# K's exponentials read from PSUM, stores of x's parts on another queue, weight blocks loaded shifted

## The chip, the cores and the metric

The kernel runs on one core of a Trainium2 chip. The metric is the device time of one execution in microseconds (us). TensorE (PE) multiplies, VectorE (DVE) and ScalarE (ACT) do arithmetic on tiles in SBUF and PSUM, GpSimd (POOL) and SyncE (SP) mostly issue DMA transfers. A name such as L457 is a line of the kernel, of the one before where nothing else is said; lines of the changed kernel lie a little further down (L457 before and L464 after are the same store).

## The reference, cut to what matters

```python
def phi(x):                                  # q, k: [8, 8, 576, 64], w_phi: [64, 128]
    proj = np.einsum('bhsd,df->bhsf', x, w_phi)
    proj = proj - np.max(np.abs(proj), axis=-1, keepdims=True)
    return np.concatenate([np.exp(proj), np.exp(-proj)], axis=-1)
q_p, k_p = phi(q), phi(k)
kv  = np.einsum('bhsf,bhsd->bhfd', k_p, v)
z   = np.sum(k_p, axis=2)
num = np.einsum('bhsf,bhfd->bhsd', q_p, kv)
den = np.einsum('bhsf,bhf->bhs', q_p, z)[..., None] + 1e-06
x   = (num / den).transpose(0, 2, 1, 3).reshape(4608, 512)

gate = 1.0 / (1.0 + np.exp(-(x @ w_gate)))   # w_gate, w_val: [512, 1536]
val  = x @ w_val
out  = (gate * val) @ w_out                  # w_out: [1536, 512]
```

A linear attention makes x, and a gated two-layer network takes x to the output. For each token (a row of 576 per head) the largest absolute value over its 128 features is taken off its projection before the exponentials of both signs. The network's weights arrive as 64-bit floats.

## The kernel before, in words

**Attention.** There are 32 steps, one for each batch and pair of heads (`attend`). A step loads q, k and v, projects K on TensorE with tokens on the partitions (L489, four 128x128 products for each of two heads) and Q with features on the partitions (L594). VectorE takes each K token's largest absolute value (L495, `mk`, one number per token). Then, for K, VectorE subtracts it from the 512 columns of a group in PSUM and writes `ek` in SBUF (L524), and ScalarE takes two exponentials of 512 elements per group, one of each sign (L536). A step has two such groups of 128x512 and a small one for the last 64 tokens. TensorE then sums K with V (L678) and multiplies by Q; VectorE's transposes (L637, L644) carry Q's maxima across partitions. Ratios of numerator and denominator, multiplied out by L809, are x, feature-major, written to the scratch `xs` in DRAM. For the first chunk of 512 tokens x is kept in SBUF and split there into a high and a low part: ScalarE writes the high part (L815), VectorE the low one (L818), four parts of 128 features each.

**First phase of the network.** x has nine chunks of 512 tokens. For the first four of the twelve blocks of 128 hidden features, each chunk goes through gate and value products (`gate`, L997: twelve matmuls of 128x512, since high and low parts give three products for each of four slices), a nonlinearity, a split of h in high (L1021) and low part, and four output products (L1054, `go` in `first_js`: twelve matmuls each, three for each of the four hidden blocks). Chunks 0 to 6 take tanh and an exponential for the sigmoid; chunks 7 and 8 take the Sigmoid function (L1017), whose table is loaded once, behind all of ScalarE's work ahead. The output product leaves PSUM through ScalarE (L1077) into one of two y buffers, from which a store (L1083) on SP's queue writes it to `out`. For chunks 1 to 8 `load_x` fetches x from `xs`, splits it, and `keep_x` (L457) stores its high and low parts to `xh` and `xl` in DRAM, for the second phase: 144 stores on SP's queue.

**Weights.** A block of weights, 128x512 numbers of 64 bits, is loaded as 32-bit words, from which VectorE and ScalarE put together high and low parts with bit operations. `weigh` does this: L855 masks, ScalarE rescales (L859), and L874, L882, L894, L911 and L946 shift, combine and multiply. There are twelve blocks for the first phase, and 24 more for the second, whose sums (`kept`) are written to DRAM scratch, partly between attention steps, partly later.

**Second phase.** The other eight blocks of hidden features go by a seven-product scheme (products of sums of blocks) over blocks of 768 tokens: L1283 multiplies, and POOL adds the results onto `out` by accumulating stores (L1437). Its first loads of x's parts (L1215) wait until all of x's parts, `xh` and `xl`, are stored.

**What sets the order.** Every operation is given to a planner (`Plan`) with its engine, a modelled duration, a rank and its buffers. The planner plays the program through with these durations and issues the operations of each engine in the order that comes out. Each engine then works strictly in that order, and a queue's transfers too. So a change of a rank, of a duration or of a count moves work on all engines. Gate products have PSUM banks of their own (three, named gate below) and attention five (named bank).

Of the kernel before, what the change touches and what calls it, by code (L numbers as in the profile page):

```python
# [8 lines left out]
F32 = mybir.dt.float32  # L9
F32R = mybir.dt.float32r  # L10
U32 = mybir.dt.uint32
# [34 lines left out]
ONPE = 12  # L46
BANKS = 5
# [4 lines left out]
WAT = 0.0  # L52
WSTEP = 6.0
# [13 lines left out]
SLACK = 12.0  # L67
LAG = 0.0
ISSUE = 0.4
# [3 lines left out]
SHARE = 0.33  # L73

# [87 lines left out]
class Plan:  # L162
# [5 lines left out]
    RATE = 0.26, 0.36  # L168
# [24 lines left out]
    def run(self):  # L193
# [33 lines left out]
        while left:  # L227
# [25 lines left out]
            free[o.eng] = t + max(o.busy, ISSUE if late and o.eng == "SP" else 0.0)  # L253
# [40 lines left out]
def attention_moe(  # L294
# [126 lines left out]
    def on_act(n, fn, reads, writes, rank, after=(), slack=0.0):  # L421
        return plan.op(
            "ACT", 0.08 + n / 1200, 0.17, fn, reads, writes, rank, None, slack, after
        )
# [26 lines left out]
    def keep_x(c, p, bufs, r):  # L451

        for n, x in enumerate(bufs):
            for t, w, of in pieces(c * CW, CW):
                sp(
                    w * 512,
                    lambda n=n, x=x, t=t, w=w, of=of: nc.sync.dma_start(  # L457
# [7 lines left out]
    def attend(i):  # L465
# [63 lines left out]

        for g in range(3):  # L530
            n = (4, 4, 1)[g] * F
            dve(n, lambda g=g: k_sub(g), [(pk[0], pk[1], pt)[g], mk[g]], [ek[g]], r + 4 + g)
# [54 lines left out]
        else:  # L587
# [59 lines left out]
            on_act(2 * S, lambda: act.activation(e(), d(), AF.Exp), [d], [e], r + 14)  # L647
# [190 lines left out]
    def weigh(j, m, r, deep, wh, wl, ms, part, after=(), again=False, whole=None):  # L838
        raw = Buf([r_raw2 if again else r_raw], [P, 2 * DM])
        top = Buf([r_top2 if again else r_top], [P, DM])  # L840

        def words(x):
            return x().rearrange("p (n two) -> p n two", two=2)

        def hi():
            return words(raw)[:, :, 1]

        sp(
            512 << 10,
            lambda: nc.sync.dma_start(raw(), w_moe[j, :, m, :].bitcast(U32)), [], [raw], r,  # L850
            after,
        )
        dve(
            DM,
            lambda: vec.tensor_scalar(top(), hi(), 0x7FFFFE00, None, op0=ALU.bitwise_and),  # L855
            [raw], [top], r, k=2.0,
# [3 lines left out]
            [], [top], r,  # L860
        )
        if deep:
            mid = Buf([r_mid], [P, 2 * DM])
            sp(
                512 << 10,
                lambda: nc.sync.dma_start(
                    mid()[:, : 2 * DM - 1].bitcast(U16),
                    w_moe[j, :, m, :].bitcast(U16)[:, 1 : 4 * DM - 1],
                ),
                [], [mid], r,  # L870
            )
            dve(
# [694 lines left out]
```

## Time and profile before

| | before |
|---|---|
| three runs, us | 1167.53, 1165.16, 1164.63 (median 1165.16) |
| the profiled execution, us | 1164.72 |
| its span in the profile, us | 1163.0 |
| mean granted TensorE clock | 0.994 |
| TensorE busy, us | 1134.9 (98%), 8940 matmuls |
| VectorE busy, us | 925.3 (80%), 1805 instructions |
| ScalarE busy, us | 712.7 (61%), 1425 instructions |
| POOL busy, us | 77.9 (7%), 94 instructions |
| DMA bytes moved | 213.37 MB, 183 GB/s on average |

The profile is of one execution; busy times are sums over the records of an engine, and issuing a DMA from SP isn't counted as busy. "Idle before" is the time that an engine stood still ahead of an instruction, with the releaser, the piece of work whose end let it go on. SPq is SP's DMA queue. The granted clock is TensorE's speed as the throttle allowed it, 1.00 being full speed.

### The profile page before, as it was taken

The numbers are of one execution on the slowest core, as the hardware profiler recorded it, in microseconds if no ns is written. First come the engines' busy times: TensorE is split into PE (matmuls) and PEld (weight loads), VectorE is DVE, ScalarE is ACT, GpSimd is POOL, SyncE is SP. The second block draws the span as 40 slices with busy tenths as digits, with TensorE's granted clock in tenths as the row PEclk, the third lists the DMA queues.
The fourth block names the chain that finished last, engine by engine and source line by source line (L and its number), as shares of the span: only waits on it lengthen the run. The fifth ranks groups of instructions, "written<-read, shape, count | busy, mean of one in ns | idle before, by whom it ended". The sixth has DMA issues, their size and how long they took to land.

```text
span 1163.0 us, 23394 instructions
## 1 busy us (share of the span) xinstructions
PE 1134.9 (98%) x8940; PEld 952.9 (82%) x8940; DVE 925.3 (80%) x1805; ACT 712.7 (61%) x1425; POOL 77.9 (7%) x94
## 2 busy tenths in 40 slices
PE   8989999999999999999989999999999999999998
PEld 6656666766676776767768999999999999999998
DVE  7998889999999999978687956756767766667665
ACT  6857676665767666553344756656567666566563
POOL 0000000000000000000000112012022022022020
PEclk9989999999999999999989999999999999999999
DMA  6773466555738548375867558468495667567671
GB/s 237 236 252 101 134 216 203 167 194 185 242 111 259 183 144 264 115 242 184 324 239 261 152 106 212 144 125 216 148 249 124 172 122 202 165 123 195 171 165 55
DMA packets 114712, 213.37 MB, mean 183 GB/s; under 512 B 21544, under 2 KB 59560, under 8 KB 114600
## 3 DMA queue, kind: packets, MB, share of 16 engines
q1 hardware_dynamic: 101928, 177.27, 46.3%
q0 software_dynamic: 12672, 34.61, 16.9%
q8 instruction: 70, 1.15, 0.4%
q14 instruction: 42, 0.34, 0.1%
HBM read 126.61 MB, written 85.07 MB: 182 GB/s over the span
## 4 chain that ended last, share of the span: by engine, by line
PE 71%; DVE 16%; DMA 7%; ACT 2%; issue 2%; SPq 2%; DVEq 0%; ACTq 0%
PE bank L1283 29%; PE gate L1283 15%; PE gate L997 8%; PE gate L1054 4%; PE bank L678 3%; DMA rb<-den 3%; PE bank L720 2%; PE bank L489 2%; DMA low<-xs 1%; PE bank L1054 1%; DVE mb L637 1%; PE bank L738 1%; PE bank L594 1%; DVE pm L616 1%; PE bank L997 1%
## 5 line engine op out<-in xcount | busy, mean ns | idle before, releaser
L1283 PE MATMUL bank<-low,high 128*128 128x384 f32 x1338 | 246.8, 336 | 0.0
L1283 PEld LDWEIGHTS bank<-low,high 128*128 128x128 f32 x1338 | 233.3, 188 | 0.9 <-DVE flat L1304 0.4
L997 PE MATMUL gate<-low 128*128 128x512 f32 x708 | 173.8, 399 | 5.4 <-ACT low L815 4.3
L997 PEld LDWEIGHTS gate<-low 128*128 128x128 f32 x708 | 131.9, 191 | 36.3 <-ACT low L815 4.8
L1283 PE MATMUL gate<-low,high 128*128 128x384 f32 x678 | 130.9, 336 | 0.6 <-ACT gate L1298 0.6
L1283 PEld LDWEIGHTS gate<-low,high 128*128 128x128 f32 x678 | 118.6, 188 | 1.1 <-ACT gate L1298 1.1
L1283 PE MATMUL bank<-low 128*128 128x384 f32 x523 | 116.8, 339 | 1.2 <-DVE spare L1304 1.0
L536 ACT ACTIVATE ek<-ek 128x512 f32<-128x512 f32 (+1 forms) x192 | 95.4, 528 | 26.5 <-DVE ek L524 25.5
L1283 PEld LDWEIGHTS bank<-low 128*128 128x128 f32 x523 | 92.7, 188 | 4.4 <-DVE spare L1304 1.3
L1054 PE MATMUL gate<-low 128*128 128x512 f32 x372 | 89.4, 394 | 0.0
L1382 ACT CAST low<-flat 128x384 fp32r<-128x384 f32 x126 | 62.8, 515 | 40.2 <-DVE flat L1391 36.7
L1054 PEld LDWEIGHTS gate<-low 128*128 128x128 f32 x372 | 68.5, 188 | 14.7 <-issue 1.0
L1437 POOL DMA_DIRECT2D out<-third x60 | 52.7, 1177 | 350.8 <-DVE third L1304 266.2
L678 PE MATMUL bank<-ek,vin 128*32 128x256 f32 x1240 | 73.2, 381 | 2.2 <-ACT d L607 2.2
L1304 DVE TENSOR_TENSOR flat<-bank,flat 128x384 f32<-128x384 f32 x74 | 40.4, 554 | 40.9 <-PE bank L1283 34.1
L678 PEld LDWEIGHTS bank<-ek,vin 128*32 128x32 f32 x1240 | 37.5, 110 | 41.6 <-issue 5.6
L1391 DVE TENSOR_TENSOR flat<-flat,bank 128x384 f32<-128x384 f32 x39 | 21.4, 550 | 61.2 <-PE bank L1283 61.2
L1437 POOL DMA_DIRECT2D out<-spare x22 | 19.4, 881 | 686.5 <-DVE flat L1376 662.9
L1283 PE MATMUL gate<-low 128*128 128x384 f32 x267 | 65.1, 338 | 0.0
L1385 DVE TENSOR_TENSOR low<-flat,low 128x384 fp32r<-128x384 f32 x108 | 58.8, 551 | 1.8 <-ACT low L1382 0.6
L1298 ACT COPY bank<-bank 128x384 f32<-128x384 f32 x81 | 37.8, 467 | 33.7 <-PE bank L1283 32.2
L1021 ACT CAST low<-flat 128x512 fp32r<-128x512 f32 x36 | 22.3, 619 | 53.0 <-DVE flat L1046 41.4
(213 smaller groups left out, 2181.4 us busy)
## 6 DMA issues: line engine op xcount, KB each, us to landing
out<-third POOLq DMA_DIRECT2D x60, 384.0 KB, 8.2
flat<-w_moe SPq DMA_DIRECT2D x28, 512.0 KB
low<-xh SPq DMA_DIRECT2D x33, 384.0 KB
low<-xl SPq DMA_DIRECT2D x33, 384.0 KB
low<-xs SPq DMA_DIRECT2D x33, 384.0 KB
kin<-k SPq DMA_DIRECT2D x32, 320.0 KB
qin<-q SPq DMA_DIRECT2D x32, 320.0 KB
vin<-v SPq DMA_DIRECT2D x32, 320.0 KB
```

What stands on the lines that cost most here:

```text
L489: nc.tensor.matmul(pk[hd]()[:, t, :], x()[head(hd), t * P : t * P + P], wk[head(hd), :], start=True, stop=True,)
L536: lambda g=g, sg=sg: act.activation(ek[g]()[:, :, sg * F : sg * F + F], ek[g]()[:, :, F:], AF.Exp, scale=1.0 - 2.0 * sg,),
L678: nc.tensor.matmul(o_[o : o + Q, : 2 * F], vx()[:, 2 * t + hd, o % D : o % D + Q], (e0, e1)[hd][:, t, :] if t < 4 else e2[:, 0, :], start= ...
L720: nc.tensor.matmul(nm()[o : o + Q, :], w()[:, sg, o : o + Q], es[sg]()[:, o // D, cs], start=sg == 0, stop=sg == 1, tile_position=(0, o),)
L997: nc.tensor.matmul(o(), a()[:, ws], x(), start=cc + n == 0, stop=cc == NC4 - 1 and n == 2,)
L1054: nc.tensor.matmul(acc(), w()[:, ms], a(), start=first and i == 0, stop=last and i == 2)
L1283: nc.tensor.matmul(o()[:, :HT], s()[:, ws], y, start=first and n + cc + i_ == 0, stop=n == len(terms) - 1 and cc == steps - 1 and i_ == 2, ...
L1298: HT, lambda: act.copy(o()[:, :HT], src()[:, :HT]), [src], [o], -200.0, before
L1304: HT, lambda: vec.tensor_tensor(at_(), p()[:, :HT], q(), op=ALU.add),
L1382: on_act(HT, lambda: act.copy(hh(), y()), [y], [hh], -100.0, after)
L1385: lambda: vec.tensor_tensor(hl(), y(), hh().bitcast(F32), op=ALU.subtract),
L1437: lambda f=f, y=y: nc.gpsimd.dma_start(final(f, dc), flat_y(y), accum_op=ALU.add),
```

## The change

It does five things, and changes some of the planner's durations and ranks besides.

1. From step 12 on (20 of the 32 steps), K's two large groups are no longer subtracted by VectorE. ScalarE reads the projection in PSUM and takes the exponential with the token's maximum as its bias, one ACTIVATE for each of four slices of 128 elements and each sign. VectorE writes the negated maxima (128x4).
2. `keep_x`'s 144 stores go through POOL's queue instead of SP's.
3. The 24 weight blocks for sums are loaded shifted by two bytes (the host pads each row by one number to allow it), so that one word holds what two words held; each block needs one combining operation of VectorE less.
4. The weights of the first phase have ranks of their own: gate and value blocks of all four hidden blocks ahead, the output blocks later. Which blocks are loaded a second time at another offset (`deep`) follows from that position.
5. For the last three chunks (`PARTED`) an output product is cut in two, three hidden blocks first (nine matmuls) and the fourth by itself (three).

```diff
-WAT = 0.0
-WSTEP = 6.0
+WG = 0.0
+WGS = 6.0
+WO = 72.0
+WOS = 6.0
...
+PARTED = 3
...
-ISSUE = 0.4
+ISSUE = 0.43
...
                 sp(
-                    w * 512,
-                    lambda n=n, x=x, t=t, w=w, of=of: nc.sync.dma_start(
+                plan.op(
+                    "POOL", 1.0, w * 512,
+                    lambda n=n, x=x, t=t, w=w, of=of: nc.gpsimd.dma_start(
...
+        def k_exp(g, sg):
+            for t in range(4):
+                act.activation(
+                    ek[g]()[:, t, sg * F : sg * F + F], pk[g]()[:, t, :], AF.Exp,
+                    bias=(mn, mk)[sg][g]()[:, t : t + 1], scale=1.0 - 2.0 * sg,
+                )
+
+        mn = [at(f"mq{g}", 2, [P, 4]) for g in range(2)]
         for g in range(3):
             n = (4, 4, 1)[g] * F
+            if i >= FUSED and g < 2:
+                plan.op(
+                    "DVE", 0.1, 0.16,
+                    lambda g=g: vec.tensor_scalar(mn[g](), mk[g](), -1.0, None, op0=ALU.mult),
+                    [mk[g]], [mn[g]], r + 4 + g,
+                )
+                for sg in range(2):
+                    plan.op(
+                        "ACT", 1.12, 0.17, lambda g=g, sg=sg: k_exp(g, sg),
+                        [pk[g], (mn, mk)[sg][g]], [(ek[g], sg)], r + 6 + g,
+                    )
+                continue
...
+    def weighed(j, m, r, mask, rings, after=(), slack=0.0, deep=True, o=1):
...
+                lambda x=x, o=at_: nc.sync.dma_start(
+                    x().bitcast(U16), w_moe[j, :, m].bitcast(U16)[:, o : o + 4 * DM]
                 ),
...
+    def weigh_whole(j, m, r, w, ms, part, after, early):
+
+        top, raw, mid = weighed(
+            j, m, r, 0x7FFF0000, (r_raw, r_top, r_raw) if early else (r_raw2, r_top2),
+            after, LATER, early and DEEP,
+        )
...
-            def go(t=t, acc=acc):
-                for i in range(JA):
-                    mm_out(acc, t, hs[i], i, i == 0, i == JA - 1)
...
+            for a, b in ((0, JA - 1), (JA - 1, JA)) if c >= NCH - PARTED else ((0, JA),):
+
+                def go(t=t, acc=acc, a=a, b=b):
+                    for i in range(a, b):
+                        mm_out(acc, t, hs[i], i, i == 0, i == JA - 1)
...
-                i, WAT + 3 * WSTEP * i, WSTEP, lambda m, i=i: 3 * i + m >= RAW, (r_wh, r_wl, r_oh, r_ol),
+                i, lambda m, i=i: WO + WOS * i if m == 2 else WG + WGS * (2 * i + m),
+                lambda m, i=i: (8 + i if m == 2 else 2 * i + m) >= RAW, (r_wh, r_wl, r_oh, r_ol),
```

How the work is ordered then, at three places. Each row is a line, an operation and its tiles, output<-input, with the output's shape; "x12" is so many in a row. First VectorE, where the first chunk's x gets its last low parts (L818 before, L845 after). Before:

```order
L946 SCALAR_TENSOR_TENSOR low<-flat 128x512
L855 TENSOR_SCALAR flat<-flat 128x512
L809 TENSOR_TENSOR xp_623<-ex_391,mb_678 128x576
L495 TENSOR_REDUCE mk_217<-bank_164 128x4
L882 SCALAR_TENSOR_TENSOR flat<-flat 128x512
L809 TENSOR_TENSOR xp_840<-ex_688,rb_517 128x576
L818 TENSOR_TENSOR low<-xp_623,low 128x512
L637 STREAM_TRANSPOSE mb_678<-pm_558 128x1152
L818 TENSOR_TENSOR low<-xp_840,low 128x512
```

After the change:

```order
L836 TENSOR_TENSOR xp_518<-ex_687,rb_478 128x576
L836 TENSOR_TENSOR xp_763<-ex_365,mb_700 128x576
L653 COPY pn_667<-pm_646 64x36
L654 COPY pn_667<-pm_646 64x36
L655 TENSOR_TENSOR pm_646<-pm_646,pn_667 128x36
L658 COPY pn_667<-pm_646 32x36 x4
L659 TENSOR_TENSOR pm_646<-pm_646,pn_667 128x36
L845 TENSOR_TENSOR low<-xp_518,low 128x512
L845 TENSOR_TENSOR low<-xp_763,low 128x512
L664 STREAM_TRANSPOSE mb_700<-pm_646 128x1152
```

Between the two divisions (L809, L836) and the low parts, work on a weight block has been replaced by small work on Q's maxima (L653 to L659), and the transpose (L637, L664) now stands behind both low parts. Second SP's queue, where chunk 6's outputs are stored. Before:

```order
L457 DMA xh<-low 128x128
L457 DMA xh<-low 128x384
L457 DMA xl<-low 128x128
L457 DMA xl<-low 128x384
L1083 DMA out<-flat 128x512 x2
L850 DMA more<-w_moe 128x1024
L1123 DMA g_98<-flat 128x1792
L850 DMA more<-w_moe 128x1024
L1083 DMA out<-flat 128x512 x2
```

After the change:

```order
L1002 DMA low<-xs 128x128
L1002 DMA low<-xs 128x384
L1119 DMA out<-flat 128x512 x4
L875 DMA more<-w_moe 128x2048 x2
L1159 DMA g_100<-staged 128x1792
L875 DMA more<-w_moe 128x2048 x2
L1252 DMA flat<-xs 128x768
```

The stores of x's parts ahead of the outputs (L1083, L1119) are gone, and the four outputs are together, behind loads of x (L1002). Third TensorE, from the last gate or value product of chunk 6 to those of chunk 7. Rows that read from high,low are chunk 7's; the rows of L1054 (L1087 after) ahead of them are chunk 6's output products. Before:

```order
L997 MATMUL gate_191<-low 128x512 x12
L997 MATMUL bank_176<-high,low 128x512 x12
L1054 MATMUL gate_178<-low 128x512 x12
L1054 MATMUL gate_185<-low 128x512 x12
L1054 MATMUL gate_191<-low 128x512 x12
L1054 MATMUL gate_178<-low 128x512 x12
L997 MATMUL bank_154<-high,low 128x512 x12
L997 MATMUL bank_166<-high,low 128x512 x12
```

After the change, from chunk 6's last two output products to chunk 7's first two:

```order
L1087 MATMUL gate_178<-low 128x512 x12
L1087 MATMUL gate_185<-low 128x512 x12
L1030 MATMUL bank_164<-high,low 128x512 x12
L1030 MATMUL bank_176<-high,low 128x512 x12
L1030 MATMUL bank_150<-high,low 128x512 x12
L1030 MATMUL bank_166<-high,low 128x512 x12
L1030 MATMUL bank_152<-high,low 128x512 x12
L1030 MATMUL gate_191<-high,low 128x512 x12
L1030 MATMUL gate_178<-high,low 128x512 x12
L1030 MATMUL gate_185<-high,low 128x512 x12
L1087 MATMUL bank_164<-low 128x512 x9
L1087 MATMUL bank_176<-low 128x512 x9
```

A whole output product is a row of x12, and of a parted one the first piece is x9. Before, one product of chunk 7 (bank_176) stood ahead of chunk 6's output products; now all eight stand behind them, and two pieces of x9 come next, ahead of the pieces that need the fourth hidden block.

More of the change, by code (lines that the diff above doesn't have):

```diff
@@ L67 @@
 SLACK = 12.0
+PARTED = 3
+LATER = 0.0
+DEEP = False
 LAG = 0.0
-ISSUE = 0.4
+ISSUE = 0.43
 SPAN = 46.0
@@ L252, in run @@
                     b.slot.take()
-            free[o.eng] = t + max(o.busy, ISSUE if late and o.eng == "SP" else 0.0)
+            free[o.eng] = t + max(o.busy, ISSUE if o.eng == "SP" else 0.0)
             if o.eng in ("SP", "POOL"):
@@ L419, in dve, with on_act @@
         )
[L421 removed]
+    def on_act(n, fn, reads, writes, rank, after=(), slack=0.0, k=1.0):
         return plan.op(
[L423 removed]
+            "ACT", 0.08 + n / 1200 / k, 0.17, fn, reads, writes, rank, None, slack, after
         )
@@ L836, in attend, with words @@
             t += wd
[L838 to L843, printed above, removed]
-        def hi():
[L846 to L852, printed above, removed]
-        dve(
-            DM,
-            lambda: vec.tensor_scalar(top(), hi(), 0x7FFFFE00, None, op0=ALU.bitwise_and),
-            [raw], [top], r, k=2.0,
+    def words(x, n):
+        return x().rearrange("p (n two) -> p n two", two=2)[:, :, n]
+    def weighed(j, m, r, mask, rings, after=(), slack=0.0, deep=True, o=1):
+        raw, top = Buf([rings[0]], [P, 2 * DM]), Buf([rings[1]], [P, DM])
+        mid = Buf([rings[2]], [P, 2 * DM]) if deep else raw
+        for x, at_ in ((raw, 0), (mid, 1)) if deep else ((raw, o),):
+            sp(
+                512 << 10,
+                lambda x=x, o=at_: nc.sync.dma_start(
+                    x().bitcast(U16), w_moe[j, :, m].bitcast(U16)[:, o : o + 4 * DM]
+                ),
+                [], [x], r, after,
+            )
+        def hi():
+            return words(raw, 1)
+        if not deep and o:
+            dve(
+                DM,
+                lambda: vec.tensor_scalar(
+                    hi(), hi(), 16, 0xFFFF0000, op0=ALU.logical_shift_left, op1=ALU.bitwise_and
+                ),
+                [], [raw], r, k=2.0, slack=slack,
+            )
+        dve(
+            DM,
+            lambda: vec.tensor_scalar(top(), hi(), mask, None, op0=ALU.bitwise_and),
+            [raw], [top], r, k=2.0, slack=slack if deep else 0.0,
         )
@@ L886, in weigh @@
         )
-        if whole is None:
-            on_act(
-                DM, lambda: act.copy(wh()[:, ms], top().bitcast(F32)), [top], [(wh, part)], r,
-            )
+        return top, raw, mid
+    def weigh(j, m, r, deep, wh, wl, ms, part):
+        top, raw, mid = weighed(j, m, r, 0x7FFFFE00, (r_raw, r_top, r_mid), (), 0.0, deep, 0)
+        on_act(
+            DM, lambda: act.copy(wh()[:, ms], top().bitcast(F32)), [top], [(wh, part)], r,
+        )
         if deep:
@@ L1103, in kept @@
         for i, j in enumerate(pair(n)):
-            o_ = weigh(
-                j, m, r + 3 * i, False, None, None, slice(2 * i * KH, 2 * (i + 1) * KH), i,
-                after + combined[-1:], not early, w,
+            o_ = weigh_whole(
+                j, m, r + 3 * i, w, slice(2 * i * KH, 2 * (i + 1) * KH), i,
+                after + combined[-1:], early,
             )
```

123 lines of the change are left out of this document (56 added, 67 removed).

## The prediction

> **What bounds the kernel now.** I read the engines' busy shares first, then busy time by stage, then the matmuls that waited in the timeline, then what the engine named there had been waiting for.
>
> ```profile
> PE 1134.9 (98%) x8940; PEld 952.9 (82%) x8940; DVE 925.3 (80%) x1805; ACT 712.7 (61%) x1425; POOL 77.9 (7%) x94
> ```
>
> TensorE is busy 98% of the span, and the change leaves its matmuls as they are in number and shape. So time can be won only where TensorE stands still or runs at half clock. The stages, with the columns us, then PE, PEld, DVE, ACT, POOL busy (instructions), granted clock, DMA share, GB/s:
>
> ```profile
> 0.00:65.00 65.00, 60.46 (x881) 42.71 (x882) 55.09 (x123) 46.37 (x99) 0.70 (x6) 1.00 0.75 242
> 65.00:92.00 27.00, 21.64 (x171) 13.71 (x174) 24.08 (x45) 17.00 (x32) 0.00 (x0) 0.87 0.70 231
> 92.00:200.00 108.00, 105.78 (x1300) 70.55 (x1292) 95.11 (x205) 74.14 (x148) 0.00 (x0) 1.00 0.53 160
> 200.00:520.00 320.00, 315.89 (x3125) 222.67 (x3121) 302.61 (x644) 203.95 (x398) 0.00 (x0) 1.00 0.60 190
> 520.00:577.00 57.00, 55.96 (x281) 43.45 (x274) 42.18 (x75) 20.68 (x35) 0.00 (x0) 1.00 0.74 253
> 577.00:616.00 39.00, 34.05 (x137) 26.81 (x136) 34.07 (x50) 18.71 (x24) 0.00 (x0) 0.91 0.70 256
> 616.00:1163.00 547.00, 541.12 (x3073) 533.06 (x3071) 372.13 (x668) 331.80 (x690) 77.18 (x88) 1.00 0.65 163
> ```
>
> Two stages stand out. From 65 to 92 us TensorE is idle 5.4 us, and a clock of 0.87 over 27 us takes another 0.13 x 27 = 3.5 us: 8.9 us (place A). From 577 to 616 it is idle 4.95 us, and 0.09 x 39 = 3.5 us go to the clock: 8.5 us (place B); the 1.0 us just ahead belongs to the same hand-over, so 9.5 us. From 92 to 520 us only 6.3 us are lost in 428, although VectorE is busy 302.6 of 320 us there: it is full, but it is not what TensorE waits for. The second phase loses 5.9 us of 547, and the first stage 4.5, most of it before the first load lands.
>
> What TensorE waited for at A and at B, in the timeline (start, us, then idle time before it and its releaser in brackets):
>
> ```profile
> 65.28 2.31 PE L997 MATMUL gate<-low 128*128 128x512 f32 x9
> 71.93 0.80 PE L997 MATMUL gate<-low 128*128 128x512 f32 x1 [4.34 <-ACT low L815]
> 73.74 7.77 PE L997 MATMUL gate<-low 128*128 128x512 f32 x23 [1.02 <-DVE low L818]
> ...
> 577.76 1.52 PE L1054 MATMUL bank<-low 128*128 128x512 f32 x6
> 580.40 0.50 PE L1054 MATMUL bank<-low 128*128 128x512 f32 x1 [1.12 <-ACT low L1021]
> 585.45 11.69 PE L1054 MATMUL bank<-low 128*128 128x512 f32 x39 [3.51 <-ACT low L1021]
> ```
>
> At A the first chunk of x lacks its last two of four parts (L815, L818), and VectorE makes them at the end of a queue that is full. At B the output product of chunk 7 lacks h of its last columns (L1021). ScalarE was late with it because of what stood ahead:
>
> ```profile
> 567.08 1.21 ACT L1077 ACTIVATE flat<-gate 128x512 f32<-128x512 f32 x2 [8.45 <-DMA out<-flat]
> 568.31 1.28 ACT L1017 ACT_TABLE_LOAD   x1
> ...
> 540.06 1.04 SPq L457 DMA_DIRECT2D xh<-high  x2
> 562.90 0.87 SPq L457 DMA_DIRECT2D xl<-low  x2
> 563.81 0.93 SPq L1083 DMA_DIRECT2D out<-flat  x2
> ```
>
> ScalarE stood 8.45 us for one of the two y buffers, whose store (L1083) sat on SP's queue behind the stores of x's parts (L457, from 540.06 to 563.77); only then came the sigmoid's table and the sigmoids (L1017).
>
> **Place A.** The order shows gate and value weights ahead of the out weights. Ahead of the third part's L818 VectorE now has one weight block less, that is one each of L855, a later mask, L882 and L946, and one small subtraction (L524) more; ahead of the fourth also one transpose (L637) less. Prices from consecutive starts:
>
> ```profile
> 71.15 0.67 DVE L818 TENSOR_TENSOR low<-xp,low 128x512 fp32r<-128x512 f32 x1
> 71.75 1.36 DVE L637 STREAM_TRANSPOSE mb<-pm 128x1152 f32<-128x1152 f32 x1
> 73.05 0.64 DVE L818 TENSOR_TENSOR low<-xp,low 128x512 fp32r<-128x512 f32 x1
> 74.29 0.41 DVE L855 TENSOR_SCALAR flat<-flat 128x512 uint32<-128x512 uint32 x1
> 74.62 0.68 DVE L946 SCALAR_TENSOR_TENSOR low<-flat 128x512 fp32r<-128x512 uint32 x1
> 75.22 1.34 DVE L644 TENSOR_TENSOR d<-d,mb 128x1152 f32<-128x1152 f32 x1
> ...
> 175.66 1.16 PE L489 MATMUL bank<-wk,kin 64*128 64x128 f32 x16
> 176.65 1.03 PE L594 MATMUL bank<-qin,wk 64*128 64x512 f32 x4
> ```
>
> A masking costs 0.33 us, a combining 0.60, a transpose 1.30. The third part comes 2 x 0.33 + 2 x 0.60 - 0.2 = 1.7 us sooner (71.82 to 70.1), the fourth 3.0 us sooner (73.69 to 70.7). TensorE has one projection of K (L489, 0.99 us) and one of Q (L594, 1.03) more ahead of the third part, so it gets there at 67.6 + 2.0 = 69.6. What is left is 0.5 us of waiting and 0.5 for the fourth part, and no stop long enough to compare with the 4.34 us behind which the clock fell. A: 8.9 less 1.0, **-7.9 us**. Bounds: -8.9 when the parts are in time; 0 when a slow divisor load takes VectorE's lead away.
>
> **Place B.** 32 stores of 0.48 us leave SP's queue; chunk 6's four outputs follow the loads of x directly, so L1077 is not held up. The order also puts eight gate products of chunk 7, 8 x 2.75 us by L997's 0.229 us per matmul, behind the last output product of chunk 6: the sigmoids have these 22 us, as before, and now start about 20 us sooner. Chunk 7's output product is cut so that 18 matmuls (4.1 us) go ahead of the ones that need the last h; behind the last value product stand a multiplication, a copy and a subtraction, some 2.0 us. B and the 1.0 us ahead of it: 9.5 less 1.5 for a queue out of step, **-8.0 us**. Bounds: -9.5, and 0 when another store or weight load holds the y buffers. The eight output products of chunks 7 and 8 still precede the second phase, so nothing is only put off.
>
> **K's exponentials.** 20 of 32 pairs change. VectorE loses two subtractions of 128x512 each and gains two negations of 128x4; ScalarE's four ACTIVATEs of 512 elements become sixteen of 128 from PSUM, each with a bias tile. The trace has no such form; the nearest rows, of ScalarE and then of VectorE's groups:
>
> ```profile
> 15.44 0.62 ACT L889 CAST low<-flat 128x512 fp32r<-128x512 f32 x1
> 15.96 0.73 ACT L859 ACTIVATE flat<-flat,ebias 128x512 uint32<-128x512 uint32 x1
> 16.59 0.26 ACT L581 ACTIVATE eq<-bank 128x128 f32<-128x128 f32 x1
> 16.74 0.60 ACT L581 ACTIVATE d<-bank 128x512 f32<-128x512 f32 x1
> ...
> 307.33 1.75 ACT L536 ACTIVATE ek<-ek 128x512 f32<-128x512 f32 x3 [1.32 <-DVE ek L524]
> ...
> L524 DVE TENSOR_TENSOR ek<-bank,mk 128x512 f32<-128x512 f32 x62 | 39.9, 681 | 0.0
> L786 DVE TENSOR_SCALAR dn<-dn 128x9 f32<-128x9 f32 x30 | 4.8, 161 | 1.0 <-DMA dn<-dr 1.0
> L911 DVE SCALAR_TENSOR_TENSOR flat<-flat 128x512 uint32<-128x512 uint32 x22 | 15.0, 687 | 0.1
> ```
>
> 128 elements from PSUM take 0.15 us from start to start, and a bias tile adds 0.63 - 0.52 = 0.11: 0.26 us, four of them 1.04, against 0.56 for 512 (1.75 less 0.63, halved). ScalarE gets 80 x 0.48 = 38 us more. Without a charge for the bias it is 80 x 0.04 = 3 us; with no overlap, 0.26 + 0.11 each, 80 x 0.92 = 74 us. [...] I keep 38, since both bias rows stand next to each other. In 200-520 ScalarE then goes from 204 to 242 of 320 us, 76%. VectorE saves 40 x (0.64 - 0.16) = 19 us there, and 24 x 0.69 = 16.5 us by the blocks for sums, which lose one combining (L911) each. That opens no time on TensorE by itself, as the stage lost 4.1 us of 320 with VectorE full. I book +1.5 us for ScalarE's longer queue; bounds -4 and +22 (the slow rival). The shifted weight loads carry the same 512 KB: 0.
>
> **Stores on POOL.** 144 stores at about the price of the accumulating ones:
>
> ```profile
> L1437 POOL DMA_DIRECT2D out<-third x60 | 52.7, 1177 | 350.8 <-DVE third L1304 266.2 <-ACT third L1432 45.0 <-ACT spare L1432 19.9
> ...
> 598.30 0.87 SPq L1215 DMA_DIRECT2D low<-xh  x1
> 616.01 3.35 PE L1283 MATMUL bank<-low,high 128*128 128x384 f32 x18
> ...
> 178.81 2.37 PE L678 MATMUL bank<-ek,vin 128*32 128x256 f32 x40 [1.13 <-ACT d L607]
> ```
>
> 144 x 1.18 = 170 us on an engine that was idle until 660. What waits for them is the first load of the second phase (L1215), which needs every store of x's parts. The last 32 begin near 540 - 8 = 532 and end at 570. From the load to the second phase's first matmul it was 17.7 us, and TensorE will get there near 616 + 11 (four output products moved ahead) - 16 = 611, so 23 us are spare. Cost 0.
>
> **Sum.** 1163.0 - 7.9 - 8.0 + 1.5 = 1148.6 us of span. The profiled execution took 1164.72 us, 1.7 more than its span, and the median of the runs shown is 0.4 above it: **1150.7 us**.
>
> **Rivals.** *ScalarE and the banks decide (slower).* A bank with K's projection was free after one subtraction; now it is held until both signs' ACTIVATEs have passed ScalarE's queue, 2.1 us plus the queue, and attention has five banks. At 178.81 us TensorE waited 1.13 us for that queue. If each of the 20 pairs costs 1.13 us, that is 22.6: 1150.7 - 1.5 + 22.6 = 1171.8. It turns slower at 15.9 / 20 = 0.8 us per pair. Against it: 24% of ScalarE stays free, and VectorE, which now feeds it, is eased.
>
> *POOL falls behind.* If a store took over (611 - 17.7 - 532) / 32 = 1.9 us, the second phase would start late; at 2.5 us it would be 19 us late and, with 3.5 us of clock, the time 1173. [...]
>
> *A or B stays:* one of the two waits is taken over by a late divisor load or by a weight load ahead of chunk 7's outputs: 1150.7 + 8 = 1158.7.
>
> *More is won:* the 6.3 us of scattered waits from 92 to 520 go with VectorE's load, and A and B vanish: 1150.7 - 1.5 - 6.3 - 2.5 = 1140.
>
> **How the numbers follow.** Forecast 0.58 (1144 to 1157 by itself), A or B stays 0.17, slower by banks 0.11, POOL 0.07, more 0.07. 0.3% is 3.5 us, about what a measurement tells from no change: faster is below 1161.7. Faster: 0.58 + 0.07 + 0.14 of A or B = 0.79; same 0.03 + 0.03 + 0.03 = 0.09; slower 0.12. The range, 1140 to 1164, goes down to the case of more and up past the one of A or B, and leaves out most of the two bad ones.
>
> **What would show it.** In the new profile the stage around 65 to 80 us should show a granted clock of 1.00 and at most 1.5 us of waiting; ScalarE's wait for out<-flat should be gone and chunk 7's output product should wait under 2 us; the second phase should start 15 to 18 us sooner once 11 us are allowed for the four output products; ScalarE's busy time should rise by 38 us and VectorE's fall by 35. A wait of matmuls for ScalarE in every pair, a stop ahead of the second phase, or POOL's stores above 1.9 us would make it wrong.

## The result

The changed kernel took 1152.07 us (median of four runs, 1150.64 to 1153.27). The kernel before took 1165.76 us in the same series (1164.63 to 1167.53). The ratio is 0.9881, with a 95% interval of 0.9863 to 0.9898: faster by 13.7 us, where 14.5 were forecast. The span of the profiled execution fell from 1163.0 to 1150.5 us.

The total is nearly the one forecast, but it is not made of the terms forecast, so that the match is in part luck. One place (B) went for the reasons given. The other (A) went for a reason that the prediction had not seen, and a new stop ahead of it gave more than half of that term back.

### The profile page after: what moved, and what is told of

The parts are those of the page before. It is cut to its first block, busy times and chain, and to the rows that moved or that the text cites. A ratio compares the mean times of both kernels' runs of the same rounds, so it can differ in the third digit from the quotient of the medians.

```text
span 1150.5 us, 23769 instructions
## 1 busy us (share of the span) xinstructions
PE 1130.5 (98%) x8940; PEld 951.8 (83%) x8940; DVE 892.9 (78%) x1781; ACT 749.8 (65%) x1665; POOL 157.9 (14%) x238
## 4 chain that ended last, share of the span: by engine, by line
PE 75%; DVE 12%; DMA 7%; ACT 3%; issue 2%; SPq 1%; POOL 0%; DVEq 0%; ACTq 0%; POOLq 0%
PE bank L1320 29%; PE gate L1320 15%; PE gate L1030 8%; PE gate L1087 5%; PE bank L747 3%; PE bank L705 3%; DMA rb<-den 3%; PE bank L1030 2%; PE bank L496 2%; DMA den<-dn 2%; PE bank L765 2%; PE bank L1087 1%; DVE mb L664 1%; PE bank L719 1%; PE bank L621 1%
## 5 line engine op out<-in xcount | busy, mean ns | idle before, releaser
L1030 PE MATMUL gate<-low 128*128 128x512 f32 x720 | 172.2, 394 | 0.0
L464 POOL DMA_DIRECT2D xh<-low x64 | 35.3, 558 | 436.0 <-ACT low L1008 284.0
L1087 PE MATMUL gate<-low 128*128 128x512 f32 x360 | 87.0, 394 | 0.0
L1474 POOL DMA_DIRECT2D out<-third x60 | 55.4, 1021 | 228.7 <-DVE third L1341 121.6
L1087 PEld LDWEIGHTS gate<-low 128*128 128x128 f32 x360 | 66.3, 188 | 14.3 <-issue 1.0
L1341 DVE TENSOR_TENSOR flat<-bank,flat 128x384 f32<-128x384 f32 x73 | 40.1, 554 | 37.1 <-PE bank L1320 30.0
L563 ACT ACTIVATE ek<-ek 128x128 f32<-128x128 f32 (+1 forms) x112 | 48.9, 456 | 13.0 <-DVE ek L531 12.0
L1474 POOL DMA_DIRECT2D out<-spare x23 | 23.7, 1292 | 238.5 <-DVE spare L1341 115.7
```

The source lines that it names most:

```text
L464: lambda n=n, x=x, t=t, w=w, of=of: nc.gpsimd.dma_start(of(xparts[n], p), x()[:, t - c * CW :][:, :w].bitcast(F32)),
L563: lambda g=g, sg=sg: act.activation(ek[g]()[:, :, sg * F : sg * F + F], ek[g]()[:, :, F:], AF.Exp, scale=1.0 - 2.0 * sg,),
L1030: nc.tensor.matmul(o(), a()[:, ws], x(), start=cc + n == 0, stop=cc == NC4 - 1 and n == 2,)
L1087: nc.tensor.matmul(acc(), w()[:, ms], a(), start=first and i == 0, stop=last and i == 2)
L1341: HT, lambda: vec.tensor_tensor(at_(), p()[:, :HT], q(), op=ALU.add),
L1474: lambda f=f, y=y: nc.gpsimd.dma_start(final(f, dc), flat_y(y), accum_op=ALU.add),
```

## The profile after

The engines' busy shares of the changed kernel:

```profile
PE 1130.5 (98%) x8940; PEld 951.8 (83%) x8940; DVE 892.9 (78%) x1781; ACT 749.8 (65%) x1665; POOL 157.9 (14%) x238
```

ScalarE rose by 37.1 us (38 forecast), VectorE fell by 32.4 (35 forecast), POOL rose by 80 (170 forecast).

The changed kernel by stage. The columns are us, then PE, PEld, DVE, ACT and POOL busy (instructions), the granted clock, DMA share and GB/s:

```profile
0.00:30.00 30.00, 25.50 (x363) 20.05 (x365) 17.62 (x41) 17.55 (x37) 0.70 (x6) 1.00 0.71 240
30.00:50.00 20.00, 17.44 (x209) 11.43 (x208) 18.46 (x41) 14.19 (x30) 2.36 (x4) 0.91 0.68 219
50.00:65.00 15.00, 13.71 (x202) 8.46 (x204) 14.36 (x34) 11.69 (x25) 2.14 (x4) 1.00 0.74 222
65.00:92.00 27.00, 26.70 (x321) 18.08 (x313) 26.34 (x49) 17.16 (x34) 4.27 (x8) 1.00 0.66 217
92.00:200.00 108.00, 106.50 (x1315) 70.18 (x1318) 98.10 (x217) 85.17 (x191) 8.58 (x16) 1.00 0.57 178
200.00:520.00 320.00, 316.68 (x3121) 222.87 (x3111) 285.61 (x644) 236.25 (x608) 44.81 (x80) 1.00 0.60 196
520.00:577.00 57.00, 57.00 (x252) 46.55 (x249) 41.30 (x71) 22.53 (x37) 17.95 (x32) 1.00 0.72 247
577.00:616.00 39.00, 39.00 (x177) 32.52 (x176) 26.22 (x33) 19.54 (x26) 0.00 (x0) 1.00 0.76 265
```

The first 65 us of the kernel before, which the prediction showed only as one row:

```profile
0.00:30.00 30.00, 25.96 (x368) 20.19 (x369) 21.46 (x47) 19.52 (x41) 0.70 (x6) 1.00 0.69 235
30.00:50.00 20.00, 19.51 (x274) 12.75 (x278) 18.85 (x44) 15.47 (x36) 0.00 (x0) 1.00 0.72 225
50.00:65.00 15.00, 14.99 (x244) 9.77 (x237) 14.78 (x34) 11.38 (x22) 0.00 (x0) 1.00 0.92 278
```

What TensorE loses in a stretch is its idle time plus the share of the stretch that the clock withheld. From 30 to 92 us after the change that is 2.56 + 1.29 + 0.30 idle and 0.09 x 20 = 1.8 of clock, 6.0 us; before it was 0.49 + 0.01 + 5.36 and 3.5, 9.4 us. The second phase took 1163.0 - 616.01 = 547.0 us before; 11.0 of them (the four output products) now stand ahead of it, which leaves 536.0 to compare. After, it starts at 613.35 and takes 537.2.

| stretch | lost before, us | lost after, us | difference | forecast |
|---|---|---|---|---|
| 0 to 30 us | 4.0 | 4.5 | +0.5 | 0 |
| 30 to 92 us (place A in it) | 9.4 | 6.0 | -3.4 | -7.9 |
| 92 to 520 us | 6.3 | 4.8 | -1.5 | +1.5 |
| 520 to 616 us (place B) | 9.5 | 0.0 | -9.5 | -8.0 |
| second phase, length | 536.0 | 537.2 | +1.2 | 0 |
| sum | | | -12.7 (span: -12.5) | -14.4 |

**Place B** is gone. ScalarE's rows for the y buffers and the sigmoid's table, and TensorE's for chunk 7's first output products and the second phase's first products:

```profile
548.02 1.29 ACT L1113 ACTIVATE flat<-gate 128x512 f32<-128x512 f32 x2 [0.74 <-DMA out<-flat]
551.86 1.28 ACT L1050 ACT_TABLE_LOAD   x1
569.81 11.06 PE L1087 MATMUL bank<-low 128*128 128x512 f32 x48
613.35 26.95 PE L1320 MATMUL bank<-low,high 128*128 128x384 f32 x152
```

The wait for out<-flat is 0.74 us instead of 8.45, the table comes at 551.9 instead of 568.3 us, and the 48 matmuls run through without a stop.

**Place A** shows no stop either, but look when x's last two low parts come. VectorE, then TensorE:

```profile
74.77 1.29 DVE L845 TENSOR_TENSOR low<-xp,low 128x512 fp32r<-128x512 f32 x2
73.90 0.94 PE L1030 MATMUL gate<-low 128*128 128x512 f32 x3
75.18 8.45 PE L1030 MATMUL gate<-low 128*128 128x512 f32 x36
```

They are done at about 75.4 and 76.1 us. Before it was 71.82 and 73.69. So they are later, not sooner; TensorE doesn't wait for them because it needs them later still. In both orders 18 of these matmuls use only the first two parts. Before, the last of the 18 was done at 67.6 us. Now 15 are done by 74.84 (nine from 56.96, three from 62.06 and the three shown), and the other three stand at the head of the row of 36, so that the third part is first needed at about 75.18 + 3 x 0.229 = 75.9 us and the fourth some 0.7 us behind it. That is 8.3 us later than before, with about half a microsecond to spare for each part.

Of these 8.3 us, 2.0 are the two projections that the order puts ahead. TensorE lost 1.3 us at 60.95 us, which the last section shows, and 4.4 us, half clock included, at a **new stop, place C**; some 0.6 us are left for small products. TensorE, with the third projection of K as its first row:

```profile
28.15 1.16 PE L496 MATMUL bank<-wk,kin 64*128 64x128 f32 x16
32.60 0.49 PE L512 MATMUL bank<-wk,kin 128*128 128x128 f32 x2 [0.57 <-ACT kv L735]
35.30 0.85 PE L747 MATMUL bank<-eq,kv 128*32 128x288 f32 x8 [1.99 <-DVE ek L531]
35.91 1.21 PE L747 MATMUL bank<-d,kv 128*32 128x288 f32 x8
36.87 1.21 PE L747 MATMUL bank<-eq,kv 128*32 128x288 f32 x8
39.44 0.67 PE L765 MATMUL gate<-d,kv 128*32 128x288 f32 x8
```

The same projection in the kernel before, with VectorE's two waits there, and then what VectorE did meanwhile after the change:

```profile
20.96 1.16 PE L489 MATMUL bank<-wk,kin 64*128 64x128 f32 x16
22.15 1.29 DVE L495 TENSOR_REDUCE mk<-bank 128x4 f32<-128x512 f32 x2 [1.23 <-PE bank L489]
27.80 0.69 DVE L882 SCALAR_TENSOR_TENSOR flat<-flat 128x512 uint32<-128x512 uint32 x1 [1.63 <-ACT flat L859]
```

```profile
23.04 0.43 DVE L894 TENSOR_SCALAR flat<-flat 128x512 uint32<-128x512 uint32 x1 [1.31 <-DMA flat<-w_moe]
26.08 0.69 DVE L903 SCALAR_TENSOR_TENSOR flat<-flat 128x512 uint32<-128x512 uint32 x1 [2.62 <-ACT flat L898]
29.34 0.69 DVE L502 TENSOR_REDUCE mk<-bank 128x4 f32<-128x512 f32 x1 [2.10 <-PE bank L496]
34.56 0.68 DVE L531 TENSOR_TENSOR ek<-bank,mk 128x512 f32<-128x512 f32 x1
```

The projection stands 7.2 us later. VectorE is idle for 1.31 + 2.62 + 2.10 = 6.0 us between 21 and 30 us, for a weight block, for ScalarE's rescaling of it and then for the projection; before it was 1.23 + 1.63 = 2.9 us. When the projection comes, K's subtraction (L531) stands in VectorE's queue among weight work, and TensorE waits 1.99 us for the bank that the subtraction frees. Behind that, eight matmuls take 0.96 us from start to start instead of 0.48: half clock until about 39 us.

**K's exponentials and POOL's stores**, with ScalarE's rows for two groups of four and the stores' group:

```profile
303.74 1.24 ACT L539 ACTIVATE ek<-bank,mk 128x128 f32<-128x128 f32 x4
304.75 1.26 ACT L539 ACTIVATE ek<-bank,mq 128x128 f32<-128x128 f32 x4
```

```profile
L464 POOL DMA_DIRECT2D xh<-low x64 | 35.3, 558 | 436.0 <-ACT low L1008 284.0 <-ACT dr L803 83.2 <-ACT low L842 67.5
```

Four exponentials take 1.01 us, 0.25 each; 0.26 was forecast. A store of x's parts takes POOL 0.56 us, half of the 1.18 of an accumulating one.

## The experiments

In all runs the kernel before was timed beside the others, between 1157.7 and 1167.7 us, so the runs are compared by their ratio to it. The changed kernel's own is 0.9881 (0.9863 to 0.9898); it was timed only in the first series, where the kernel before had a median of 1165.76 us, against 1161.87 to 1163.31 in the later ones. A difference of some 3 us from its ratio is therefore not read. The losses are of one profiled execution of each kernel.

| run | ratio (95%) | lost from 30 to 92 us | lost from 520 to 616 us |
|---|---|---|---|
| kernel before | 1 | 9.4 | 9.5 |
| changed kernel | 0.9881 (0.9863-0.9898) | 6.0 | 0.0 |
| e1 stores on SP again | 0.9895 (0.9858-0.9933) | 6.3 | 0.0 |
| e2 products uncut | 0.9939 (0.9918-0.9959) | 5.8 | 2.2 |
| e3 old order of weights | 0.9897 (0.9870-0.9925) | 5.5 | 0.0 |
| e4 old duration in the first phase | 0.9936 (0.9914-0.9958) | 7.2 | 0.0 |
| e5 less VectorE work | 0.9891 (0.9870-0.9912) | 6.9 | 0.0 |
| e6 more VectorE work | 1.0204 (1.0172-1.0236) | 6.2 | not at the same place |
| e7 no exponentials from PSUM | 0.9902 (0.9872-0.9932) | 6.0 | 0.0 |
| e8 before, stores on POOL | 0.9947 (0.9929-0.9964) | 11.5 | 1.0 |
| e9 weight loads on POOL | 0.9909 (0.9880-0.9938) | 5.8 | 0.0 |
| e10 e4 with weight loads on POOL | 0.9927 (0.9905-0.9948) | 11.3 | 0.0 |
| e11 e6, planned for | 1.0028 (1.0006-1.0049) | 6.2 | 0.2 |
| e12 before, two edits | 0.9940 (0.9918-0.9962) | 13.3 | 0.8 |

### Place B: the queue or the order

**e1**, the queue alone put back:

```diff
-                    lambda n=n, x=x, t=t, w=w, of=of: nc.gpsimd.dma_start(
+                    lambda n=n, x=x, t=t, w=w, of=of: nc.sync.dma_start(
```

> The changed kernel with the 144 stores of x's parts issued on SyncE's queue again, at the places of the same order; every other engine's order is that of the changed kernel. Theory 'queue' (place B went because the y buffers' stores no longer wait behind the stores of x's parts): ScalarE waits again for out<-flat near 560 us, the sigmoids come late, and some 8 us come back: 1160. Rival 'order' (place B went because all eight gate and value products of chunk 7 now stand behind chunk 6's outputs, so that the sigmoids have 22 us of cover wherever the stores go): 1152, within 2 us of the changed kernel's 1152.1.

Place B stays away. ScalarE's rows of this run:

```profile
548.79 0.60 ACT L1113 ACTIVATE flat<-gate 128x512 f32<-128x512 f32 x1 [1.02 <-DMA out<-flat]
550.09 0.60 ACT L1113 ACTIVATE flat<-gate 128x512 f32<-128x512 f32 x1 [0.70 <-DMA out<-flat]
552.25 1.28 ACT L1050 ACT_TABLE_LOAD   x1
```

In this order the four stores of y stand early among the stores of x's parts (from 545.81 to 550.74 us on SP's queue, with one, four and one of the others between them), and ScalarE waits 1.02 and 0.70 us instead of 8.45. So the queue isn't needed once the order is the new one.

**e8**, the queue alone changed in the kernel before, with its old order:

```diff
-                    lambda n=n, x=x, t=t, w=w, of=of: nc.sync.dma_start(
+                    lambda n=n, x=x, t=t, w=w, of=of: nc.gpsimd.dma_start(
```

> The kernel before in its own order, with the 144 stores of x's parts issued on GpSimd's queue and nothing else changed. Theory 'queue' (with the queue free, the y buffers' stores leave at once and ScalarE reaches the sigmoids in time): the wait for out<-flat near 558 us goes and place B with it, 8 to 9.5 us: ratio 0.992 to the kernel before. Rival 'order' (in that order the output products of chunk 7 come too early for the sigmoids anyhow): place B stays, ratio 1.000.

By stage, places A and B of this run:

```profile
65.00:92.00 27.00, 21.65 (x195) 14.29 (x183) 24.38 (x43) 16.14 (x29) 6.01 (x11) 0.87 0.68 231
577.00:616.00 39.00, 38.72 (x173) 31.91 (x172) 35.31 (x54) 20.16 (x28) 0.00 (x0) 1.00 0.73 263
```

Place B is gone here too (0.28 us idle), and place A is there as before. The gain of the whole run, some 6 us by the ratio, is smaller than B and short of what I expected. This execution lost 2.1 us more from 30 to 92 us than the kernel before; the rest stays open. Either the queue or the order is enough for B; the change has both.

**e2**, the output products whole again (the first piece issues nothing):

```diff
-                    for i in range(a, b):
+                    for i in range(0 if b == JA else b, b):
```

> The changed kernel with the output products of the last three chunks whole again: the piece of nine matmuls issues nothing and the piece of three issues all twelve; all else is in the same order. Theory (the cut only hides the last h of chunk 7, some 2 us): TensorE waits about 2 us at chunk 7's first output product, no half clock, 1154. Rival (the cut is what removed place B): the long stop with its clock comes back, 8 to 9.5 us, 1160 to 1162.

In 520 to 616 us TensorE waits 2.2 us in all, with no half clock. The longest wait, at chunk 8's output product:

```profile
607.54 0.73 PE L1087 MATMUL gate<-low 128*128 128x512 f32 x2 [1.23 <-DVE low L1056]
```

The size holds: the cut hides about 2 us, and without it place B doesn't come back. The place was another: 1.2 us are at chunk 8, 0.9 at chunk 6 (539 to 540 us), and chunk 7's 48 matmuls run through. The whole run took longer by more than that, 2.6 us by the medians and 6.7 by the ratios; what these stages don't show of it stays open.

### Place A: what removed it

**e3**, the old order of the first phase's weights:

```diff
-                i, lambda m, i=i: WO + WOS * i if m == 2 else WG + WGS * (2 * i + m),
+                i, lambda m, i=i: 6.0 * (3 * i + m),
-                lambda m, i=i: (8 + i if m == 2 else 2 * i + m) >= RAW, (r_wh, r_wl, r_oh, r_ol),
+                lambda m, i=i: 3 * i + m >= RAW, (r_wh, r_wl, r_oh, r_ol),
```

> The changed kernel with the first phase's weight blocks in the old order (gate, value and output block of one hidden block after the other). Theory (place A went because one block less stands ahead of the first chunk's last low parts): the stop near 72 us and the half clock behind it come back, 8.6 us: 1160.7, granted clock near 0.87 from 65 to 92 us. Rival (place A went with the planner's other constants or with VectorE's lighter load): 1152, within 2 us.

The stop at A does not come back; TensorE is busy in all 27 us from 65 to 92 at full clock. My theory for place A falls: place A stays away without the new order of the weights. Place C is there as well, with the same 2.56 us.

**e4**. What moved the third projection of K? In the planner's order it goes back to its old place when ScalarE's rescaling of a first-phase weight block has its old modelled duration (`k=0.8` makes it longer):

```diff
-            [], [top], r, k=0.8,
+            [], [top], r, k=0.8 if mask == 0x7FFF0000 else 1.0,
```

> The changed kernel, with the planner's longer duration for ScalarE's rescaling (factor 0.8) kept only for the 24 blocks for sums; the twelve blocks of the first phase are modelled as in the kernel before. The order then has the third step's projection of K ahead of the second step's products of Q again. Theory (the new stop from 32 to 39 us, 2.6 us of waiting and some 2 us of half clock, comes from that projection standing 7 us later): the stop goes and 4 to 5.5 us with it: 1147 to 1148. Rival (TensorE then waits elsewhere for the same full VectorE, or place A comes back): 1152 to 1160.

Place C went (0.3 us lost from 30 to 50 us), but nothing was won; the run took longer. VectorE, ScalarE and TensorE of this run:

```profile
56.12 0.43 DVE L894 TENSOR_SCALAR flat<-flat 128x512 uint32<-128x512 uint32 x1 [2.42 <-DMA flat<-w_moe]
56.58 0.72 ACT L898 ACTIVATE flat<-flat,ebias 128x512 uint32<-128x512 uint32 x1 [2.48 <-DVE flat L894]
57.72 0.90 PE L731 MATMUL gate<-ident,kvt 128*128 128x128 f32 x3 [2.52 <-ACT kvt L726]
```

The stop has moved to 55 us. VectorE stands 2.42 us at the head of its queue for a weight block, ScalarE stands behind VectorE, and TensorE behind ScalarE. So the constant sets where TensorE stops, and the rival of this run was right. Place A has only 0.44 us of waiting here, though there is no place C: held up at 55 us, TensorE is done with the 18 matmuls of the first two parts at about 74.4 us, 7 us later than before the change.

**e5**. Is VectorE's load in this stage the cause? Here 30 of its operations on the weights are left out, in the same order, so that the weights lack their signs and some low bits:

```diff
-            lambda: vec.scalar_tensor_tensor(
-                top(), hi(), 0x80000000, top(), op0=ALU.bitwise_and, op1=ALU.bitwise_or
+            lambda: mask == 0x7FFF0000 and vec.scalar_tensor_tensor(
+                top(), hi(), 0x80000000, top(), op0=ALU.bitwise_and, op1=ALU.bitwise_or
...
-                lambda: vec.tensor_scalar(
+                lambda: None and vec.tensor_scalar(
```

> The changed kernel in the same order, with 30 of VectorE's operations on the twelve weight blocks of the first phase left out (the twelve that put the sign in, twelve maskings and six combinings of low bits): 12 x 0.60 + 12 x 0.33 + 6 x 0.60 = 14.8 us less of VectorE between 14 and 90 us, and weights that lack their signs and some low bits. New theory (VectorE's full queue in the first 92 us sets what TensorE loses there, and the order only moves the place): the 4.2 us of waiting from 30 to 92 us and the half clock behind them nearly all go, 4 to 5.5 us: 1147. Rival (the stop at 32 to 39 us comes from the third projection of K standing behind other TensorE work, so that VectorE is idle ahead of it whatever it has to do): the stop stays, 1151 to 1152.

No. With 14 us less to do, VectorE simply waits, and TensorE behind it, at 37.75 us instead of 35.30:

```profile
37.07 0.43 DVE L894 TENSOR_SCALAR flat<-flat 128x512 uint32<-128x512 uint32 x1 [2.88 <-DMA flat<-w_moe]
37.75 0.69 PE L765 MATMUL gate<-eq,kv 128*32 128x288 f32 x8 [2.88 <-DVE ek L531]
```

One weight block's arrival holds the queue, and a small subtraction of K stands behind it.

**e9** and **e10** took 14 of the 18 weight loads off SP's queue, in the changed kernel's order and in e4's:

```diff
-                lambda x=x, o=at_: nc.sync.dma_start(
+                lambda x=x, o=at_: queue(mask).dma_start(
+    def queue(mask):
+        loads.append(mask)
+        return nc.gpsimd if mask == 0x7FFFFE00 and len(loads) > 4 else nc.sync
```

> The changed kernel in the same order, with the first phase's weight loads after the first four (14 of 18) issued on GpSimd's queue instead of SyncE's. Theory 'queue' (in the first 92 us VectorE stands behind a weight block whose load waited on SyncE's queue behind the divisors' small transfers, and K's subtractions stand behind VectorE): the blocks land sooner, and of the 5.9 us that TensorE loses from 30 to 92 us, half clock included, 3 to 4 us go: 1147 to 1149. Rival 'buffers' (a load starts only when one of two raw buffers comes free, whatever the queue): the waits stay, 1151 to 1152.

> The order of the run with the planner's old duration for the first phase's rescaling (there TensorE stopped 2.5 us at 55 to 58 us, while VectorE waited 2.4 us for a weight block's load, and ran at half clock behind it), with the same 14 weight loads on GpSimd's queue. Theory 'queue': the 2.4 us of VectorE's wait go, TensorE's stop with its clock, 5 to 6 us: 1148 to 1150. Rival 'buffers': that stop stays, 1153 to 1155.

Neither gained. In e9, POOL's row for the first such load, and TensorE's at place C:

```profile
20.25 1.42 POOL L881 DMA_DIRECT2D flat<-w_moe  x1 [18.94 <-DVE low L956]
35.72 0.69 PE L747 MATMUL bank<-eq,kv 128*32 128x288 f32 x8 [1.99 <-DVE ek L531]
```

The load waits for L956, VectorE's last operation on the block two earlier, because there are two raw buffers. In the changed kernel the same load leaves SP's queue at 19.54 us. So SP's queue wasn't what held it. In e10 the stop near 57 us is gone, but TensorE stops at two other places:

```profile
47.70 0.90 PE L731 MATMUL gate<-ident,kvt 128*128 128x128 f32 x3 [2.65 <-ACT kvt L726]
75.59 0.80 PE L1036 MATMUL gate<-low 128*128 128x512 f32 x1 [3.04 <-ACT low L842]
```

The second one is place A again. Its expectation had tied the fate of one stop to one queue; from 30 to 92 us the run lost more, 11.3 us.

### VectorE's relief and K's exponentials

**e7**, K's exponentials as before in all steps:

```diff
-FUSED = 12
+FUSED = 99
```

> The changed kernel with K's exponentials done as before in all steps (subtraction by VectorE, two exponentials of 512 elements by ScalarE); planned anew, so that the order after step 12 moves a little. Theory (the exponentials from PSUM buy nothing and cost at most 1.5 us): 1150 to 1152. Rival 'banks' (they hold the banks and cost TensorE time in each step): 1148 or less. Rival 'relief' (VectorE's time there is worth something): 1156 or more.

The ratio is 0.9902, and its interval overlaps the changed kernel's. From 200 to 520 us:

```profile
200.00:520.00 320.00, 318.33 (x3124) 225.17 (x3117) 304.36 (x649) 206.67 (x400) 43.28 (x80) 1.00 0.59 193
```

VectorE has 19 us more and ScalarE 30 less than in the changed kernel, and TensorE's idle time is 1.7 us against 3.3. The exponentials from PSUM buy nothing that these runs show. Their cost in this stage is 1.6 us in one execution of each kernel, too little for the ratios to show.

**e6**, VectorE's relief given back as repeated work in the same order:

```diff
-                    lambda g=g: vec.tensor_scalar(mn[g](), mk[g](), -1.0, None, op0=ALU.mult),
+                    lambda g=g: (
+                        maxima(mk[g](), pk[g](), 4),
+                        vec.tensor_scalar(mn[g](), mk[g](), -1.0, None, op0=ALU.mult),
+                    ),
...
-            lambda: vec.tensor_tensor(
+            lambda: [vec.tensor_tensor(
                 w()[:, ms], top().bitcast(F32), words(mid, 0).bitcast(F32), op=ALU.add
-            ),
+            ) for _ in range(2)],
```

> The changed kernel in the same order with VectorE's relief given back: the maxima of K are taken twice in the 20 changed steps (40 x 0.60 us) and the last addition of the 24 weight blocks for sums is done twice (24 x 0.57), 38 us more of VectorE, as busy as before the change. Theory (VectorE's relief after 92 us opened no time on TensorE): 1152 to 1154, the idle time of TensorE from 92 to 520 us stays under 7 us. Rival (the relief is part of the gain): 1157 or more, with the waits of before in 92 to 520 us.

This was far from what I expected: some 38 us more than the changed kernel by the ratios. From 200 to 520 us by stage, and then the two largest of TensorE's waits there (us in total, times, longest):

```profile
200.00:520.00 320.00, 296.78 (x2799) 205.48 (x2795) 291.54 (x635) 220.52 (x573) 34.90 (x64) 0.97 0.53 172
```

```profile
PE bank L768 <- ACT ek L539: 13.3, 9, 2.0
PE bank L750 <- ACT d L632: 4.2, 5, 1.4
```

TensorE is idle 23.2 us, VectorE 28.5: none of them is full. TensorE waits for K's exponentials (L539) 13.3 us in nine waits; in the program these take VectorE's maxima and their negation as the bias, and the repeated maxima stand in that chain.

**e11**, the same work, with its duration known to the planner:

```diff
-                    "DVE", 0.1, 0.16,
+                    "DVE", 0.7, 0.16,
...
         return dve(
-            DM,
+            2 * DM,
```

> The run with VectorE's extra work (maxima twice, last additions twice, 38 us), but the planner knows the longer durations, so that the order is made for them. Theory 'load' (between 200 and 520 us VectorE then has 319 of 320 us to do, and no order hides that): 1180 to 1190, as in the unplanned order. Rival 'order' (the 36 us came from an order made for shorter operations): 1155 to 1162.

The ratio falls from 1.0204 to 1.0028: about 20 of the 38 us came from an order made for shorter operations, and some 17 remain. Both expectations missed. In this stage:

```profile
200.00:520.00 320.00, 306.60 (x2974) 215.08 (x2970) 302.22 (x663) 232.84 (x602) 42.81 (x80) 0.99 0.55 180
```

VectorE is about as busy as in e7 (302 against 304 us), yet TensorE loses 13.4 us against 1.7. The difference is ScalarE (233 against 207 us) and that the work lies in K's chain. Which of the two weighs more stays open. For the change it says that, with the exponentials on ScalarE, VectorE has not 38 us to spare in this chain.

### Two edits alone

**e12**, the kernel before with the stores on POOL's queue and only the planner's longer duration:

```diff
-                    lambda n=n, x=x, t=t, w=w, of=of: nc.sync.dma_start(
+                    lambda n=n, x=x, t=t, w=w, of=of: nc.gpsimd.dma_start(
...
-        on_act(
-            DM, lambda: act.activation(top(), top(), AF.Relu, bias=ebias, scale=8.0),
+        plan.op(
+            "ACT", 0.08 + DM / 960, 0.17,
+            lambda: act.activation(top(), top(), AF.Relu, bias=ebias, scale=8.0),
             [], [top], r,
```

> The kernel before with two edits of the change and nothing else: the stores of x's parts on GpSimd's queue, and the planner's longer duration (factor 0.8) for ScalarE's rescaling of weight blocks, by which the third projection of K falls behind the sums of K with V as in the changed kernel. K's exponentials, the shifted blocks, the new ranks of weights and the cut output products are all as before. Theory (place B went with the queue, and the first stage gained with the order that this constant sets; the other parts buy nothing): 8 to 9.5 us for B and 3 to 4 for the first stage, 1151 to 1153 where the kernel before takes 1163, a ratio of 0.989 to 0.991. Rival (the other parts carry a third of the gain): no better than the queue alone, ratio 0.995.

Place C appears, as in the changed kernel, and in e8, without the longer duration, it does not; so this constant alone makes it. But a second stop follows:

```profile
34.81 1.19 PE L720 MATMUL bank<-eq,kv 128*32 128x288 f32 x8 [1.99 <-DVE ek L524]
74.05 0.80 PE L509 MATMUL bank<-qin,wk 128*128 128x128 f32 x2 [3.76 <-DMA qin<-q]
```

Here it is a load of q that comes late, and the clock is 0.87 from 65 to 92 us as at place A. The run gains what the queue alone gained, as the rival said. So the 3.4 us from 30 to 92 us need something else of the change too. The planner's duration of an issue on SP (ISSUE, 0.43 us, which now holds during attention as well, where before it was 0.06), the exponentials' duration (`k=0.88`), and the new form of the weights' operations are left; they weren't tried one by one.

## Why the prediction was right, and where it was not

- **TensorE is the bound, only stops and clock can be won: right.** Idle time fell from 28.1 to 20.0 us, and the mean granted clock rose from 0.994 to 0.998, which is 7.0 against 2.3 us. Together that is 12.8 us, the 12.5 us of span within rounding.
- **Place B, -8.0: right in its mechanism, measured -9.5.** The term was short by the 1.5 us set aside for a queue out of step. The prediction put both reasons side by side, the free queue and the order of products and stores; e8 and e1 show that each is enough. The cut of the products hides 2.2 us of it (e2), about the forecast size, but at chunks 6 and 8.
- **Place A, -7.9: wrong in its mechanism and its size.** The step that failed is "The third part comes 2 x 0.33 + 2 x 0.60 - 0.2 = 1.7 us sooner (71.82 to 70.1), the fourth 3.0 us sooner (73.69 to 70.7)". They came 3.6 and 2.4 us later. I counted what stands directly ahead of the parts in the two orders and let VectorE's queue arrive there at its old time. It had been idle for 6.0 us between 21 and 30 us, where before it was 2.9. TensorE's arrival, forecast for 69.6 us, came at 75.9, chiefly because it had lost 4.4 us at C and 1.3 us at 60.95. So the stop at A went because TensorE was later, by more than the parts were. In two orders without place C, TensorE stands elsewhere: at 55 us in e4, and at 45 us and again at A for 3.04 us in e10. From 30 to 92 us the gain was 3.4 us. Which part of the change makes this gain stays open (e12).
- **The first 65 us had no term.** The prediction said of them only that most of their 4.5 us lie ahead of the first load. The planner's longer duration for ScalarE's rescaling moved the third projection of K there by 7 us (it starts at 28.15 us, and with the old duration at 22.64 in e4; in e12 this duration alone takes it to 27.66). The order could have shown it; I had compared the orders at A and B alone.
- **K's exponentials: right.** 38 us were forecast for ScalarE and 37.1 came; 0.26 us for one exponential and 0.25 came. The stage from 92 to 520 us lost 1.5 us less than before, where 1.5 more was booked. That doesn't clear the exponentials: e7, without them, lost 3.4 us there against 4.8, so the booked cost may be real and the gain be of other parts of the change. That VectorE's relief "opens no time on TensorE by itself" holds for the 19 us of e7. It does not hold for 38 us in K's chain (e6, e11).
- **Stores on POOL: cost 0 as forecast,** at half the assumed price (0.56 against 1.18 us), so the rival that POOL falls behind was far off. The stores stayed at 0.56 us on average beside a VectorE that was busy 41 of 57 us from 520 to 577 us.
- **The second phase** started 2.66 us sooner (616.01 to 613.35) with 11 us of output products ahead of it, so 13.7 sooner; 15 to 18 were forecast. The forecast had no loss at place C (4.4 us); the larger gains at B and from 92 to 520 us made up only part of it.

That the total was nearly right is luck, because two misses met: place A with the new stop gave 4.5 us less than booked, and B with the stage from 92 to 520 us gave 4.5 more. Another 1.7 us went in the first 30 us and in the second phase, for reasons that no run here shows.

## What to carry to other kernels

Where a planner or scheduler sets the order, a changed duration anywhere moves work everywhere: compare the two orders along the whole bottleneck engine, not only at the stops that the old profile shows. A stop removed is proved only when what it waited for comes sooner; if it comes later and the stop is gone, the waiting engine was held up elsewhere. Repeating an operation in place prices a relief only together with the order made for it, since e6 and e11 differ by some 20 us for the same work.

## What the runs showed of the hardware

Shorter stops than expected were followed by the half clock. The prediction compared with a stop of 4.34 us. Here it came behind 1.99 us, with 0.57 us of waiting and a short piece of work ahead of them (place C: half clock until about 39 us, about 3.4 us long). A stop of 2.52 us (e4) was followed by about 6.8 us of half clock, as was the one of 4.34 us before the change, while 2.65 us (e10) and 2.88 us (e5) were followed by about 3.3 and 3.4 us, and 1.29 us in the changed kernel by none; its row, with the matmuls behind it at 0.5 us a group:

```profile
60.95 0.69 PE L747 MATMUL bank<-eq,kv 128*32 128x288 f32 x8 [1.29 <-ACT kv L735]
61.46 0.67 PE L747 MATMUL bank<-d,kv 128*32 128x288 f32 x8
```

So the length of the stop alone doesn't tell.
